# A new hand-written order for the start of a fused attention and squared-ReLU kernel, without its second set of zero matmuls

## The chip, the cores and the metric

The kernel runs on one core of one Trainium2 chip. The metric is device time in microseconds for one launch; the time before is the median of three runs. A profile is one further execution, with its own time.

The engines are named as the profile names them: PE (matmuls), ACT, DVE and POOL (elementwise work), SP (which here only issues DMAs). POOL also issues all loads that change fp32 to bf16 on the way.

## What is computed

```python
# attention: batch 4, 8 heads, sequence 768, head size 64; n_global 8, n_local 96
scores = (q @ k.T) / sqrt(64) + bias          # bias: minus slope times distance, per head
scores = where(first 8 keys, or 0 <= i - j < 96, scores, -1e9)
a = softmax(scores);  attn = a @ v
x = attn.transpose(0, 2, 1, 3).reshape(3072, 512)
# two-layer block
out = relu(x @ w_in) ** 2 @ w_out             # w_in 512 x 2048, w_out 2048 x 512
```

All inputs and the output are fp32 in DRAM; the matmuls run in bf16 and accumulate in fp32.

## The kernel before

**Tiles and stages.** The 3072 tokens are 24 tiles of 128, six to a batch element, and two tiles make a block (12 blocks). For each tile j the kernel transposes q and k (`tr.0.j`, `tr.1.j` on PE, then the copies `T.0.j`, `T.1.j` out of PSUM), computes the scores (`sc.j.0`) of its own keys and of the tile before, takes exp (`exp.j.odd.g` on ACT), multiplies with v (`pv.j.half`), normalizes (`norm`, DVE) and transposes x (`trx.j` on PE, copy `xT.j`). From tile 8 on the transposes are DMAs on SP's queue. For tiles 0 to 2 the bias is put into the scores by matmuls (`bias.j.0`); for later tiles the exps are multiplied with a table (`mul`, DVE). The eight global keys and rows of v are copied from tile to tile within a batch element (`gk.j`, `gv.j`).

**The two layers.** Blocks 0 and 1 do the first layer plainly (`s1.block.step`, then `relu` and `sq`). Blocks 2 to 11 do it with seven instead of eight products over sums of halves (`h.block.group.p1` to `p7`, with copies `u` on ACT and additions `c` on DVE). Blocks 1 to 11 do the second layer the same way (`s2.block.p1` to `p7`, with sums `sum`, weight sums `wsum`, `isum`, copies `part`, outputs `o`, stores `st`); block 0 does it plainly (`s2.0.step.half`).

**Who sets the order.** The program is recorded as a list of named operations, and the text ORDER (lines 57 to 161) gives the order in which they are issued, one word each. `name@V`, `@A`, `@P` chooses DVE, ACT or POOL; digits behind a colon are the PSUM banks (eight in all) that the operation opens. Each engine works through its own instructions in this order, and semaphores make it wait for data and for buffers. Operations on different engines overlap; a word's place counts only against words on the same engine. `ld.*` and `load.j` are loads on POOL's queue, `st.*` and `T.8` to `T.23` stand on SP's queue.

**The start.** q and k of tile 0 come as fp32 over SP (lines 313 to 324) and are transposed as fp32. Eight matmuls on zeros (lines 371 and 372, NWARM) run before anything has landed. A second set of eight (NKEEP, lines 529 to 533, the word `warm`) stands between tile 0's q and k transposes. POOL's first loads are piece 3 of w_in, k and q of tile 1, v of tile 0. q and k of tiles 1 to 5, all of v up to tile 5, w_in (ten transfers) and w_out (eight) are loaded once; `load.6` and later bring v, q and k of one tile each.

**The places that the change touches**, with the lines of the kernel before: `open_sc` and `emit_sc` (568, 590), which give the score matmuls their banks; the dependencies of `pv` (758 to 760); the ring of copies `u` (897, 973); and the last block's final product `p3`, which is cut into 192 and 64 columns, each with its own addition `o.11.p3` and store (1200, 1261, 1281).

```python
for i in range(NWARM):
    nc.tensor.matmul(out=banks[7], lhsT=zero[:, :P], rhs=zero, start=True, stop=True)
```

## Time and profile before

| | us |
|---|---|
| time, median of 3 runs | 199.85 |
| the three runs | 199.13, 199.85, 200.0 |
| the profiled execution's own time | 199.37 |
| its span, from its first to its last instruction | 197.6 |
| PE busy in the span | 191.9 |
| DVE busy | 173.2 |
| ACT busy | 163.0 |
| POOL busy | 80.4 |

The span is what the trace covers; 199.37 - 197.6 = 1.77 us of the execution's time lie around it. Times in the rows are microseconds from the span's start. A row of the timeline gives start, duration, engine, line, operation, output and inputs with their shape, the count of merged instructions, and in brackets the idle time before it with what ended that. A matmul's duration includes its passage through the array, so two matmuls in a row overlap: the distance between their starts is what one of them costs, not the duration. An engine that the row names as a releaser is the one that was last to arrive.

### The profile page before, as it was taken

The page shows a single profiled execution, that of the slowest core. Times are in us where ns is not written, and L with a number is a line of the kernel's source. Part 1 is how long each engine was busy: PE and PEld are TensorE (multiplying, and loading weights), DVE is VectorE, ACT ScalarE, POOL GpSimd, SP SyncE. Part 2 cuts the span into 40 slices and gives each one's busy share as a digit, 9 for nine tenths or more (in the row PEclk, how much of TensorE's full clock was granted, in tenths as well). Part 3 has the DMA queues.
Part 4 walks back from the last instruction along what each step waited for, and adds up shares of the span by engine and source line. Part 5 has one row for each costly group of instructions (what it writes and reads, how often), then busy time and mean ns, then how long its engine had stood idle before and what let it go on. Part 6 is the DMA issues. An engine that isn't in the chain of part 4 may idle for free.

```text
span 197.6 us, 6777 instructions
## 1 busy us (share of the span) xinstructions
PE 191.9 (97%) x2776; PEld 169.6 (86%) x2776; DVE 173.2 (88%) x423; ACT 163.0 (82%) x335; POOL 80.4 (41%) x101
## 2 busy tenths in 40 slices
...
GB/s 127 153 158 171 181 181 185 182 202 159 139 209 191 75 200 88 145 174 210 151 129 203 114 124 194 160 121 92 136 81 116 154 55 56 27 30 163 0 106 106
DMA packets 111857, 26.91 MB, mean 136 GB/s; under 512 B 103379, under 2 KB 109011, under 8 KB 111827
## 3 DMA queue, kind: packets, MB, share of 16 engines
...
q8 instruction: 21, 0.34, 0.6%
...
## 4 chain that ended last, share of the span: by engine, by line
PE 95%; DVE 2%; issue 1%; ACT 0%; DVEq 0%
PE bank L1212 35%; PE bank L950 32%; PE bank L1061 7%; PE bank L599 6%; PE bank L748 5%; PE bank L1339 4%; PE bank L372 2%; PE bank L506 2%; PE bank L532 1%; DVE qkT L433 1%; PE bank L816 1%; PE bank L579 0%; ACT qkT L429 0%; DVE o L1287 0%; DVE v L433 0%
## 5 line engine op out<-in xcount | busy, mean ns | idle before, releaser
L1015 ACT ACTIVATE hs<-hr 128x512 bf16<-128x512 f32 x72 | 44.8, 641 | 5.1 <-DVE hr L995 4.7
L665 ACT ACTIVATE esc<-bank 128x512 bf16<-128x512 f32 x78 | 42.9, 614 | 1.3 <-PE bank L599 1.0
L1212 PE MATMUL bank<-wsum,hsum 128*128 128x256 bf16 x264 | 36.2, 273 | 0.0
L1212 PEld LDWEIGHTS <-hsum 128*128 128x128 bf16 x360 | 32.1, 98 | 4.1 <-issue 0.5
L995 DVE CUSTOM_DVE_ANT_0 hr<-bank,early 128x512 f32<-128x512 f32 x45 | 30.4, 685 | 2.5 <-PE bank L950 1.5
L950 PEld LDWEIGHTS <-win 128*128 128x128 bf16 x480 | 29.7, 98 | 1.0
L950 PEld LDWEIGHTS <-qk_first 128*128 128x128 bf16 x480 | 29.7, 98 | 1.0
L429 ACT COPY early<-bank 128x512 f32<-128x512 f32 x42 | 24.5, 591 | 3.6 <-PE bank L950 3.3
L690 DVE TENSOR_TENSOR at<-esc,E 128x1024 bf16<-128x1024 bf16 x39 | 26.7, 696 | 0.1
L1212 PEld LDWEIGHTS <-hs 128*128 128x128 bf16 x264 | 24.0, 98 | 2.6
L310 POOL DMA_DIRECT2D qk<-in_q_dram x18 | 16.0, 890 | 21.9 <-DMA qkT<-qk 20.6
L1212 PE MATMUL bank<-wout,hs 128*128 128x256 bf16 x176 | 24.9, 273 | 0.0
L310 POOL DMA_DIRECT2D v<-in_v_dram x18 | 16.0, 888 | 18.3 <-DVE v L480 14.9
L950 PE MATMUL bank<-xT,win 128*128 128x128 bf16 x320 | 23.4, 219 | 0.0
L431 POOL COPY v<-v 8x520 bf16<-8x520 bf16 x8 | 5.7, 718 | 43.3 <-PE bank L748 43.3
L950 PE MATMUL bank<-xs,qk_first 128*128 128x128 bf16 x320 | 22.8, 219 | 0.0
L779 DVE TENSOR_TENSOR x<-bank,rs 128x256 bf16<-128x256 f32 x48 | 20.4, 425 | 1.7
L865 ACT ACTIVATE hr<-bank 128x512 f32<-128x512 f32 x33 | 19.4, 598 | 1.3 <-PE bank L950 0.4
L748 PE MATMUL bank<-v,at 128*128 128x65 bf16 x352 | 17.8, 193 | 0.0
L1287 DVE TENSOR_TENSOR o<-bank,part 128x256 f32<-128x256 f32 (+2 forms) x34 | 13.8, 410 | 3.3 <-PE bank L1212 3.2
L429 ACT COPY part<-bank 128x256 f32<-128x256 f32 x29 | 10.9, 375 | 7.1 <-PE bank L1212 6.9
L310 POOL DMA_DIRECT2D qk<-in_k_dram x18 | 16.1, 897 | 0.9 <-DMA win<-in_moe_w_in_dram 0.5
...
## 6 DMA issues: line engine op xcount, KB each, us to landing
out_dram<-o SPq DMA_DIRECT2D x22, 256.0 KB, 2.5
v<-in_v_dram POOLq DMA_DIRECT2D x24, 128.0 KB, 5.6
qk<-in_q_dram POOLq DMA_DIRECT2D x18, 128.0 KB, 5.0
qk<-in_k_dram POOLq DMA_DIRECT2D x18, 128.0 KB, 5.8
wout<-in_moe_w_out_dram POOLq DMA_DIRECT2D x8, 256.0 KB, 8.5
win<-in_moe_w_in_dram POOLq DMA_DIRECT2D x6, 256.0 KB, 6.9
qk_first<-in_k_dram POOLq DMA_DIRECT2D x5, 128.0 KB, 5.6
qk_first<-in_q_dram POOLq DMA_DIRECT2D x5, 128.0 KB, 5.7
```

The source lines that it names most:

```text
L310: nc.gpsimd.dma_start(out=dst, in_=src)
L429: nc.scalar.copy(dst, src)
L665: nc.scalar.activation(out=tiles[tag, j, g][:, odd], in_=tiles.pop(("sc", j, odd, g)).rearrange("p a c -> p (a c)"), func=Act.Exp, scale=s ...
L690: nc.vector.tensor_mul(at, tiles.pop(("esc", j, g)), bias)
L748: nc.tensor.matmul(out=po[:, hi, :], lhsT=tiles["at", j, g][:, odd, at * P : (at + 1) * P], rhs=v_sb[kj][:, h, :], start=(i == 0), stop=(i ...
L779: nc.vector.tensor_tensor(out=x[:, 4 * hf : 4 * hf + 4, :], in0=po[:, :, :D], in1=rs.to_broadcast([P, 4, D]), op=Alu.mult,)
L865: nc.scalar.activation(dst, src, Act.Relu)
L950: nc.tensor.matmul(out=tiles["h", blk, g, bank][:, n], lhsT=left_[:, s, k], rhs=right_[:, k], start=opens and n == 0 and k == 0, stop=k == ...
L995: nc.vector._custom_dve(TENSOR_ADD_SAT, out=hr, in0=src, in1=tiles.pop(("u", blk, g, i)), s0=float("inf"), s1=0.0,)
L1015: nc.scalar.activation(hs, hr, Act.Square)
L1061: nc.tensor.matmul(out=hT[:, c, cols], lhsT=w_in_sb[s][:, kt, c * P : (c + 1) * P], rhs=tiles["xT", blk][:, kt, cols], start=(kt == 0), st ...
L1212: nc.tensor.matmul(out=tiles["acc", blk, bank][:, cols], lhsT=left_[:, s], rhs=right_[:, cols], start=first and s == 0, stop=s == NSTEP - ...
```

## The change

The second set of zero matmuls goes. In ORDER, all words up to tile 7's transposes stand in a new order: POOL's loads begin with q and k of tile 1 and follow the tiles, with w_in and w_out behind; the bias matmuls, transposes, scores, exps and first-layer products of blocks 0 and 1 are interleaved anew, and some copies, ReLUs and squares change between ACT, DVE and POOL (the copies `gv.2` to `gv.4` leave POOL). Behind that the order of the engines' work stays nearly as it was, with other bank numbers and with loads and stores grouped at fewer places.

In the code: the score matmuls can open several banks from an offset; a copy `u` takes a buffer from a list of free ones and gives it back; `pv` of tile j also waits for the load of v of tile j-1; and in the last block both additions of `p3` wait until both cuts of the product are done (`done[-1]`), so that the matmuls of the second cut stand before the first addition. Lines of the changed kernel lie about seven lower than before.

```diff
--- before
+++ after
@@ -55,109 +55,109 @@
 ORDER = """
-tr.0.0:0 warm:7 tr.1.0:1 T.1.0@V bias.0.0:23 T.0.0@A sc.0.0 ld.win.3.0 exp.0.0.0 ld.k.1 tr.1.1:4 bias.1.0:5670 T.1.1@V ld.q.1
-tr.0.1:1 ld.v.0 exp.0.1.0 T.0.1@V sc.1.0 exp.1.0.1 pv.0.0:2 ld.q.2 tr.0.2:3 norm.0.0 ld.k.2 T.0.2@V ld.k.3 exp.1.1.1
-pv.0.1:4 tr.1.2:1 bias.2.0:7203 ld.v.1 norm.0.1 exp.1.1.0 ld.q.3 tr.1.3:6 gk.1@A T.1.2@A sc.2.0 exp.1.0.0 T.1.3@V
-ld.k.4 pv.1.0:4 ld.v.2 gk.2@V exp.2.1.0 exp.2.1.1 norm.1.0 trx.0:1 xT.0@A ones.6 pv.1.1:5 tr.0.3:6 T.0.3@V exp.2.0.0
-tr.1.4:2 ld.win.6.0 sc.3.0:4361 ld.q.4 norm.1.1 ld.v.3 trx.1:7 gv.1@V exp.2.0.1 exp.3.0.0 pv.2.0:5 exp.3.1.0 exp.3.0.1
-T.1.4@V xT.1@V pv.2.1:0 ld.k.5 ld.win.2.0 exp.3.1.1 gk.3@A ld.win.2.1 norm.2.0 s1.0.3:2 mul.3.0 s1.0.6:4 ld.win.4.0
-tr.0.4:7 ld.q.5 ld.v.4 norm.2.1 mul.3.1 relu.0.6@A s1.0.3#2 gv.2@P pv.3.0:3 norm.3.0 trx.2:5 T.0.4@A pv.3.1:6
-ld.win.1.0 norm.3.1 ld.win.0.1 xT.2@A sc.4.0:1047 exp.4.1.1 exp.4.1.0 tr.1.5:3 T.1.5@A s1.0.2:5 trx.3:6 xT.3@V
-ld.win.0.0 ld.win.5.0 s1.0.2#2 s1.0.2#3 s1.0.2#4 relu.0.3@V exp.4.0.1 ld.v.5 gv.3@P exp.4.0.0 gk.4@V sq.0.6@V
-relu.0.2@A s1.1.3:7 ld.win.7.0 relu.1.3@A load.6 s1.1.6:0 mul.4.1 tr.0.5:6 mul.4.0 sq.0.3@V s1.1.2:3 T.0.5@A ld.wout.3
-pv.4.0:2 ld.wout.1 sq.0.2@V sc.5.0:4157 ld.wout.0 s1.0.4:6 relu.1.2@A exp.5.1.1 s1.0.1:3 sq.1.3@A exp.5.0.0 relu.0.4@V
-s1.1.4:7 ld.wout.2 norm.4.0 pv.4.1:4 gv.4@P norm.4.1 sq.0.4@A load.7 exp.5.1.0 sq.1.2@A relu.1.4@A s1.0.0:6 gate.9
-ld.wout.4 mul.5.0 s1.0.0#2 sq.1.4@A s1.0.0#3 s1.1.5:2 trx.4:1 exp.5.0.1 relu.1.6@V s1.1.1:4 ld.wout.5 s1.0.1#2
-relu.1.1@A E0.1 mul.5.1 relu.1.5@A pv.5.0:7 s1.1.7:0 s1.1.0:5 sq.1.1@V norm.5.0 ld.wout.6 E0.0 sq.1.5@V tr.1.6:4
-sq.1.6@A pv.5.1:2 relu.1.7@A tr.0.6:7 s1.0.0#4 norm.5.1 xT.4@A sq.1.7@A h.2.0.p2:0 ld.wout.7 T.1.6@V h.2.1.p2:1
-trx.5:2 xT.5@V relu.1.0@A sq.1.0@A gate.14 h.2.0.p1:5 xs.2.0 s1.0.5:4 sum.1.2 s1.0.7:2 relu.0.1@A xs.2.1 gate.10
-sum.1.0 sum.1.1 relu.0.0@A T.0.6@A sc.6.0:36 wsum.0.0 sum.1.3 sq.0.0@A sq.0.1@A s2.0.0.0:7 relu.0.7@A s2.0.1.0 load.9
...
+ld.q.1 ld.k.1 ld.k.2 ld.q.2 ld.v.0 ld.q.3 ld.k.3 ld.v.1 ld.k.4 ld.v.2 ld.q.4 ld.v.3 ld.win.3.0 ld.win.6.0 ld.win.2.0
+ld.win.2.1 ld.k.5 ld.q.5 ld.v.4 ld.win.0.0 ld.win.0.1 tr.0.0:0 T.0.0@V ones.6 load.6 ld.v.5 ld.win.4.0 ld.win.1.0
+ld.win.7.0 ld.win.5.0 ld.wout.3 ld.wout.0 ld.wout.1 ld.wout.2 load.7 ld.wout.4 ld.wout.5 ld.wout.6 ld.wout.7 tr.1.0:1
+T.1.0@A bias.0.0:23 tr.0.1:4 T.0.1@V sc.0.0 exp.0.0.0 exp.0.1.0 tr.1.1:5 T.1.1@V bias.1.0:6701 tr.1.2:4 T.1.2@A sc.1.0
+gk.1@V exp.1.0.0 exp.1.1.0 exp.1.1.1 tr.0.2:2 T.0.2@V bias.2.0:5346 pv.0.0:2 pv.0.1:7 sc.2.0 exp.1.0.1 norm.0.0
+exp.2.1.1 norm.0.1 tr.0.3:1 exp.2.1.0 tr.1.3:0 trx.0:2 T.1.3@V exp.2.0.1 pv.1.0:7 pv.1.1:6 gate.9 exp.2.0.0 gk.2@V
+xT.0@V tr.1.4:3 T.0.3@V T.1.4@A norm.1.0 gv.1@V sc.3.0:0241 exp.3.1.0 pv.2.0:5 norm.1.1 norm.2.0 pv.2.1:7 tr.0.4:3
+gk.3@A exp.3.0.1 norm.2.1 exp.3.0.0 trx.1:6 trx.2:2 T.0.4@V sc.4.0:5470 exp.3.1.1 mul.3.0 gv.2@A pv.3.0:3 xT.1@A
+gk.4@A mul.3.1 norm.3.0 pv.3.1:1 s1.0.3:6 s1.0.3#2 exp.4.0.0 norm.3.1 exp.4.1.1 xT.2@A exp.4.0.1 trx.3:5 xT.3@A
+gate.11 relu.0.3@V s1.0.6:3 exp.4.1.0 mul.4.0 s1.0.2:0 s1.1.3:1 gv.3@A s1.0.2#2 sq.0.3@V tr.1.5:2 s1.0.2#3 relu.0.6@V
+s1.0.2#4 tr.0.5:7 relu.0.2@V s1.1.6:6 pv.4.0:5 T.1.5@V T.0.5@A sq.0.6@A sc.5.0:4307 mul.4.1 relu.1.3@A pv.4.1:2
+norm.4.0 exp.5.1.0 s1.0.0:1 s1.0.0#2 exp.5.0.1 exp.5.1.1 exp.5.0.0 sq.1.3@V sq.0.2@V s1.0.0#3 s1.0.0#4 s1.1.0:5
+relu.1.0@A sq.1.0@A s1.1.2:3 norm.4.1 tr.0.6:0 relu.1.2@A relu.1.6@A tr.1.6:7 load.9 load.8 T.8 trx.4:4 gv.4@V T.0.6@A
+mul.5.0 pv.5.0:2 mul.5.1 pv.5.1:5 xT.4@V T.1.6@V gate.13 sc.6.0:34 E0.1 norm.5.0 gate.15 sq.1.6@V norm.5.1 relu.0.0@V
+sq.0.0@A s1.0.4:6 s1.0.1:7 s1.0.1#2 s1.1.1:0 sq.1.2@A exp.6.0.0 relu.0.1@A sq.0.1@A s1.1.7:2 h.2.1.p1:5 relu.0.4@A
+relu.1.7@A exp.6.1.0 E0.0 trx.5:1 relu.1.1@V sq.1.1@A s1.1.5:3 sq.1.7@V s1.0.7:7 xT.5@V mul.6.0 relu.0.7@A relu.1.5@V
+sq.1.5@A h.2.1.p2:6 gate.14 wsum.0.0 wsum.1.0 h.2.0.p1:0 gate.10 wsum.2.0 s2.0.0.1:2 s2.0.1.1 xs.2.0 sq.0.4@A s1.1.4:4
+s2.0.0.0:1 s2.0.2.1 s2.0.1.0 xs.2.1 s1.0.5:7 relu.1.4@A sq.1.4@A sum.1.0 tr.1.7:3 gate.12 tr.0.7:4 load.10 isum.0.0
+s2.0.2.0 isum.1.0 isum.0.1 relu.0.5@A s2.0.3.1 isum.1.1 u.2.1.1@A c.2.1.c11 pv.6.0:7 T.1.7@A s2.0.3.0 s2.0.4.0
+u.2.0.1@A norm.6.0 isum.3.0 xs.2.2 sq.0.7@A sum.1.1 h.2.0.p6 sum.1.2 sq.0.5@A h.2.0.p2:3 c.2.0.c11 isum.3.1 h.2.1.p6
+s2.0.5.0 u.2.0.2@A s2.0.4.1 s2.0.5.1 u.2.1.2@A h.2.0.p7 u.2.0.3@A s2.0.6.0 T.0.7@A s2.0.6.1 s2.0.7.1 o.0.1@A st.0.1
+T.9 load.12 T.10 load.11 sc.7.0:6743 exp.7.0.0 wsum.0.1 s2.0.7.0 wsum.2.1 s2.1.p2.0:2 s2.1.p2.1 s2.1.p1.0:6 exp.7.1.0
...
-part.11.p6@A s2.11.p2.0:6 st.10.1 s2.11.p2.1 sum.11.2#2 o.11.p2 s2.11.p7.0 s2.11.p7.1 part.11.p7@A sum.11.3 s2.11.p5.0
-s2.11.p5.1 o.11.p5 st.11.1 st.11.0 sum.11.3#2 s2.11.p4.0 s2.11.p4.1 o.11.p4@A st.11.1#2 s2.11.p3.0 s2.11.p3.1
-s2.11.p3.0#2 o.11.p3 s2.11.p3.1#2 st.11.0#2 o.11.p3#2 st.11.0#3
+sum.11.2 s2.11.p6.1 part.11.p6@A s2.11.p2.0:6 s2.11.p2.1 sum.11.2#2 o.11.p2 s2.11.p7.0 s2.11.p7.1 part.11.p7@A
+sum.11.3 s2.11.p5.0 s2.11.p5.1 o.11.p5 st.11.1 st.11.0 sum.11.3#2 s2.11.p4.0 s2.11.p4.1 o.11.p4@A st.11.1#2 s2.11.p3.0
+s2.11.p3.1 s2.11.p3.0#2 s2.11.p3.1#2 o.11.p3 st.11.0#2 o.11.p3#2 st.11.0#3
@@ -276,7 +276,6 @@
     NSUM = 2
     NAT, NESC = 4, 2
     NWARM = 8
-    NKEEP = 8
     NLATE, NO = 2, 3
     CUT = 3 * d_model // 4
     TWO = (0, 2)
@@ -526,12 +525,6 @@
             first_reads.append(tr)
             if not fp:
                 qk_users[slot(j)].append(tr)
-        if j == 0:
-            def emit_warm(e):
-                for _ in range(NKEEP):
-                    nc.tensor.matmul(out=psum(), lhsT=zero[:, :P], rhs=zero, start=True, stop=True)
-
-            plan.op(("warm",), {"PE": 0.216 * NKEEP}, emit_warm, key=base)
         if j >= JQK:
             def emit_dT(e, j=j, T_=T_):
                 nc.sync.dma_start_transpose(
@@ -565,8 +558,8 @@
             ]
             return [(*x, odd) for x in every if x[0] in gs for odd in range(2)]
 
-        def open_sc(gs, j=j):
-            for n, (g, odd) in enumerate((g, odd) for g in gs for odd in range(2)):
+        def open_sc(gs, at=0, j=j):
+            for n, (g, odd) in enumerate(((g, odd) for g in gs for odd in range(2)), at):
                 tiles["sc", j, odd, g] = psum(n).rearrange("p (a c) -> p a c", a=4)
 
         def emit_bias(e, gs, j=j, first=first, todo=todo, open_sc=open_sc):
@@ -587,13 +580,14 @@
                 )
                 opened.add((odd, g))
 
-        def emit_sc(e, gs, j=j, todo=todo, open_sc=open_sc):
+        def emit_sc(e, gs, at=0, j=j, todo=todo, open_sc=open_sc):
             if isinstance(gs, list):
                 for f, gs in gs:
-                    f(e, gs)
+                    f(e, gs, at)
+                    at += 2 * len(gs)
                 return
             if j >= NBIAS:
-                open_sc(gs)
+                open_sc(gs, at)
             for g, pair, at, kt, odd in todo(gs):
                 half = slice(odd * D, (odd + 1) * D)
                 nc.tensor.matmul(
@@ -757,7 +751,7 @@
             g = 0 if first else hf
             deps = [*mul[g], land["v", j]]
             if not first:
-                deps.append(glob.get(("v", j - 1)))
+                deps += [glob.get(("v", j - 1)), land["v", j - 1]]
             p_ = plan.op(
                 ("pv", j, hf), {"PE": 0.13 if first else 0.25}, emit_pv, deps=deps,
                 key=base + 2 + 2 * hf,
@@ -895,7 +889,7 @@
                 )
 
     u_ring = [early[:, i] for i in range(3)] + [const([P, 4 * P], FP32, f"u_{i}") for i in range(3, NU)]
-    u_next = [0]
+    u_free = list(u_ring)
 
     def first_seven(blk):
         husers = hs_users[blk] = []
@@ -971,8 +965,7 @@
                 cu = []
 
                 def emit_u(e):
-                    u = u_ring[u_next[0] % NU]
-                    u_next[0] += 1
+                    u = u_free.pop(0)
                     any_copy(e, u, tiles["h", blk, g, bank].rearrange("p a c -> p (a c)"))
                     tiles["u", blk, g, i] = u
 
@@ -992,9 +985,9 @@
                     hr = work.tile([P, 2, 2 * P], FP32, name="hr", tag="hr", bufs=NHR).rearrange("p a c -> p (a c)")
                     src = tiles["h", blk, g, bank].rearrange("p a c -> p (a c)")
                     if i:
-                        nc.vector._custom_dve(
-                            TENSOR_ADD_SAT, out=hr, in0=src, in1=tiles.pop(("u", blk, g, i)), s0=float("inf"), s1=0.0,
-                        )
+                        u = tiles.pop(("u", blk, g, i))
+                        nc.vector._custom_dve(TENSOR_ADD_SAT, out=hr, in0=src, in1=u, s0=float("inf"), s1=0.0)
+                        u_free.append(u)
                     else:
                         any_relu(e, hr, src)
                     tiles["hr", blk, g, name] = hr
@@ -1258,7 +1251,7 @@
                 copied[name] = (o, cu)
             else:
                 sub, n, other = {"p2": (0, 0, "p1"), "p5": (1, 1, "p7"), "p4": (1, 0, None), "p3": (0, 1, "p6")}[name]
-                for o, cols in zip(done, cuts):
+                for o, cols in zip([done[-1]] * len(cuts), cuts):
                     later.append((blk, name, bank, sub, n, cols, other, o, key, copied, users, prev, ousers, stores))
                 if name == "p5":
                     continue
```

172 lines of the change are left out of this document (84 added, 88 removed).

## The prediction

> **What bounds the kernel now.** First the page's busy line and its chain, then the windows, then the chain in order of time for the spacing of matmuls.
>
> ```profile
> span 197.6 us, 6777 instructions
> PE 191.9 (97%) x2776; PEld 169.6 (86%) x2776; DVE 173.2 (88%) x423; ACT 163.0 (82%) x335; POOL 80.4 (41%) x101
> ...
> PE 95%; DVE 2%; issue 1%; ACT 0%; DVEq 0%
> ```
> ```profile
> 10.00:15.00 5.00, 4.33 (x73) 3.55 (x70) 2.73 (x8) 3.54 (x9) 5.00 (x8) 1.00 2.33 160
> 15.00:20.00 5.00, 4.66 (x94) 4.26 (x91) 4.56 (x19) 4.88 (x11) 5.00 (x8) 1.00 2.06 171
> 20.00:25.00 5.00, 5.00 (x87) 4.52 (x84) 4.25 (x12) 4.60 (x10) 5.00 (x8) 1.00 1.84 180
> 25.00:30.00 5.00, 5.00 (x80) 4.56 (x78) 3.33 (x9) 4.35 (x9) 3.89 (x6) 1.00 1.81 180
> 30.00:60.00 30.00, 30.00 (x372) 24.22 (x371) 29.18 (x69) 26.11 (x53) 17.61 (x22) 1.00 1.68 179
> 21.00:193.90 172.90, 172.90 (x2547) 156.09 (x2544) 159.59 (x369) 148.77 (x304) 60.23 (x73) 1.00 1.20 134
> ```
> ```profile
> 44.43 1.30 PE bank L1339 x6
> ...
> 93.10 3.13 PE bank L950 x56
> ...
> 161.76 2.18 PE bank L1212 x20
> ```
> The window columns are busy time of PE, PEld, DVE, ACT, POOL. From 21.0 to 193.9 us PE has no gap, and its matmuls follow each other at 0.056 us for 128 columns, 0.109 for 256 and 0.217 for 512, so those 172.9 us are work, not disguised waiting. What can be saved lies before 21 us and behind 193.9. How PE starts:
>
> ```profile
> 1.19 3.60 PE L372 MATMUL bank<-early 128*128 128x512 bf16 x8 [1.19 <-DVE early L361]
> ...
> 4.58 1.06 PE L506 MATMUL bank<-ident,plain 128*128 128x128 f32 x4
> ...
> 5.43 2.62 PE L532 MATMUL bank<-early 128*128 128x512 bf16 x8
> ...
> 6.71 0.15 PEld L532 LDWEIGHTS <-early 128*128 128x128 bf16 x1 [0.28 <-issue]
> 7.03 0.53 PEld L532 LDWEIGHTS <-early 128*128 128x128 bf16 x3 [0.16 <-issue]
> ...
> 7.89 0.60 PE L506 MATMUL bank<-ident,plain 128*128 128x128 f32 x4
> ...
> 9.28 0.40 PE L599 MATMUL bank<-qkT 64*128 64x128 bf16 x8 [0.34 <-DVE qkT L433]
> ...
> 11.62 0.23 PE L599 MATMUL bank<-qkT 64*128 64x128 bf16 x2 [0.52 <-DVE qkT L433]
> ...
> 16.65 0.23 PE L599 MATMUL bank<-qkT 64*128 64x128 bf16 x2 [0.29 <-DVE qkT L433]
> ...
> 21.04 0.23 PE L599 MATMUL bank<-qkT 64*128 64x128 bf16 x2
> ```
> The eight matmuls of L372 stand 0.43 us apart ((4.58-1.19)/8), twice the later 0.217; weight loads of L532 are still far apart at 6.71 and stand close from 7.03 on. So PE runs at half speed until about 6.9 us, after 5.7 us without a gap. The page's clock row shows none of this; the spacing does. The rows of L599 are the scores of tiles 0, 1, 3 and 4 (9.28, 11.62, 16.65, 21.04).
>
> From the end of the k transposes (8.3) to 21.0 the order holds 10.5 us of PE work, counted from its matmuls by the spacings above (with 0.55 to 0.67 for a score block and 0.24 for a probabilities-times-v block of eight), in 12.7 us: 2.2 us are waits. After those transposes PE thus has 10.5 + 172.9 = 183.4 us of work.
>
> **The zero matmuls.** They take PE from 5.43 to 7.89, 2.46 us. But the transposes behind them need tile 0's k:
>
> ```profile
> plain<-in_q_dram SPq DMA_DIRECT2D x1, 256.0 KB, 3.1
> plain<-in_k_dram SPq DMA_DIRECT2D x1, 256.0 KB, 6.0
> win<-in_moe_w_in_dram POOLq DMA_DIRECT2D x1, 256.0 KB, 5.7
> ...
> 1.25 0.56 SPq L319 DMA_DIRECT2D plain<-in_k_dram  x1
> 1.34 0.89 POOL L307 DMA_DIRECT2D win<-in_moe_w_in_dram  x1 [0.17 <-issue]
> 2.22 0.90 POOL L307 DMA_DIRECT2D qk_first<-in_k_dram  x1
> 3.10 0.90 POOL L307 DMA_DIRECT2D qk_first<-in_q_dram  x1
> ```
> k landed at 1.25 + 6.0 = 7.25, beside the first piece of w_in at 1.34 + 5.7 = 7.04; if that stays, removing the matmuls gains 0.64 us. q, issued 0.6 us ahead of POOL's first transfer, took 3.1, so k can be no earlier than about 4.4. In the changed kernel the first POOL transfer is a q tile, half as large. I take 6.4 (estimate, nearer to the late end, because the sharing stays), so transposes from 6.4 to 7.1, the first of them still at half speed, against 8.3: 1.2 us earlier. A gap-free PE would then end its work at 7.1 + 183.4 = 190.5 instead of 193.9. That is the most the change could give, 3.4 us; the rest is what takes it back.
>
> **The clock.** With the zeros gone PE idles from 5.43 to about 6.4. I take it that speed still doubles near 6.9, since PE has worked 4.2 us before the gap. The other bound: the 5.7 us of gapless work start again at 6.4, half speed until 12.1. That is a rival below.
> The Trainium skill, "TensorE: Matmul & The Clock Gate", section "Part 1: The HAM clock gate", says the clock is released after one busy window of about 3.4 us, in windows that run free of the kernel's start, so that the place of the change varies from run to run. The trace agrees as far as it goes: 5.7 us lies between one window and two. By that page the gap of 1 us can spoil a window in some runs, and then the rival's price is due.
>
> **The loads.** POOL issues them in order, and they land evenly:
>
> ```profile
> qk_first<-in_k_dram POOLq DMA_DIRECT2D x5, 128.0 KB, 5.6
> ...
> qk<-in_k_dram POOLq DMA_DIRECT2D x2, 128.0 KB, 7.5
> ...
> 33.42 0.88 POOL L310 DMA_DIRECT2D qk<-in_k_dram  x1
> ...
> 36.33 0.70 POOL L307 DMA_DIRECT2D wout<-in_moe_w_out_dram  x1 [0.56 <-DMA wout<-in_moe_w_out_dram]
> 37.61 0.71 POOL L307 DMA_DIRECT2D wout<-in_moe_w_out_dram  x1 [0.58 <-DMA wout<-in_moe_w_out_dram]
> ```
> A q, k or v tile costs the queue 0.87 us (issues 0.87 apart at a steady 5.6 to land), a 256 KB weight piece 1.28 (two issues, each released by a landing), half a piece about 0.7. Tile 7's k came at 33.42 + 7.5 = 40.9. The new order starts with a 0.87 transfer in place of a 1.28 one: first landing 6.4 to 6.7 (7.04 less 0.4, and some sharing). Behind it and up to tile 7's k stand 21 tiles, 10 pieces and 4 halves: 18.3 + 12.8 + 2.8 = 33.9, so 40.3. Ahead of the transposes of that k the new order has 30.6 us of work after tile 0's transposes, so 183.4 - 30.6 = 152.8 remain: no end before 40.3 + 152.8 = 193.1. The same sum gives 192.6 for w_in piece 5 (32.6 + 160.0) and 191.4 for piece 6. Loads alone hold back 2.6 of the 3.4 us.
>
> **The order of work up to tile 7.** What must keep up is ACT and DVE:
>
> ```profile
> 17.31 2.12 ACT L665 ACTIVATE esc<-bank 128x512 bf16<-128x512 f32 x4
> ...
> 18.33 0.62 POOL L431 COPY v<-v 8x520 bf16<-8x520 bf16 x1
> ...
> 20.14 0.58 ACT L429 COPY qkT<-bank 128x512 bf16<-128x512 bf16 x1
> ```
> Four exps take 2.12, so one costs ACT 0.5. Between tile 1's first exp and the copy of tile 6's transposed q the new order gives ACT 36 instructions, about 17 us at such paces, while PE has 19.4 us of work from tile 0's transposes to tile 6's scores (before, 28.0 with about 23 on ACT). Walking the queues from 6.4: scores of tile 1 at 9.6 (11.62), of tile 3 at 14.0 (16.65, held by the DVE copy of tile 3's q), of tile 4 at 16.9 (21.04, though with less work ahead), of tile 6 at 28.8, because ACT does relu and square of block 1 before that copy. At tile 6's scores 19.4 us of counted work lie behind 7.1, so 2.3 us of waits have come up: end at 190.5 + 2.3 = 192.8. Loads give 193.1; the later decides. 193.9 - 193.1 = 0.8 us gained, 1.1 if the loads are 0.3 sooner; I take 1.0.
> The three copies of the global v rows that POOL gave up before tile 5 (0.62 each) go to ACT twice and DVE once, and are in that walk; POOL's loads are free of them. In all 16 instructions come to DVE and 12 leave it, about 2.3 us; DVE's idle time from 10 to 30 us (2.27 + 0.44 + 0.75 + 1.67 = 5.1) covers them. If that cover is gone they cost up to 2.3.
>
> **The last bank.**
> ```profile
> 194.16 0.36 DVE L1287 TENSOR_TENSOR o<-bank,part 128x192 f32<-128x192 f32 x1 [0.84 <-PE bank L1212]
> 194.57 0.28 PE L1212 MATMUL bank<-wout,hsum 128*128 128x64 bf16 x4 [0.45 <-DVE o L1287]
> 194.88 0.22 DVE L1287 TENSOR_TENSOR o<-bank,part 128x64 f32<-128x64 f32 x1 [0.37 <-PE bank L1212]
> ```
> PE waits 0.45 for DVE and DVE then 0.37 for PE. With all matmuls first, the 192-column add starts some 0.1 later and the 64-column one follows at once, 194.7 instead of 194.88; but the two stores issue one after the other. Between -0.1 and +0.3, I take 0.1 gained. The list of free u buffers, the added wait for tile j-1's v (landed long before) and the loads and stores that stand elsewhere in POOL's and SP's queues after 45 us I cost at nothing: PE's gap-free stretch covers them; without that cover a transfer that comes late would cost its lateness in full.
>
> **Sum.** 1.0 + 0.1 = 1.1 off a span of 197.6: 196.5. The profiled execution took 199.37, 1.77 around its span; so 198.3 by it. The median shown is 199.85, 0.48 above that execution; I give the result half of that: 198.5.
>
> **Rivals.**
> 1. *The clock stays low* until 9 to 12 us (0.27). For it: PE needed 5.7 gapless us. Against: 4.2 us come before the gap. Tile 1's biases and scores then run at half speed and its scores begin at about 11.0, not 9.6, with the exps and all behind them 1.4 later, over the loads' bound: end 194.3, 0.4 later than now and 0.1 back at the tail: 199.7 by the profiled run; with 12.1 another 1.0, 200.7.
> 2. *Nothing comes through* (0.13): k of tile 0 still lands at 7.25 and every load half a microsecond later than I reckon, or the exps' chain costs 1 more. For it: the new order meets its loads with 0.1 to 0.6 us to spare, where the old one had 0.7 and more. 199.2 to 199.9.
> 3. *DVE becomes the bound* (0.15), the one that makes it slower. Between 30 and 60 us it is busy for 29.18 of 30 now. If the 2.3 us are not worked off before 30, only 0.8 of idle time is left to take them, and PE, whose banks DVE frees, falls 1.5 behind: 200.9. It decides as soon as DVE shows 30.0 of 30 and PE rows are released by DVE there.
>
> **Chances.** The forecast (0.45) has its own range of 197.7 to 199.0, from the 3.4 us that are not to be had in full and the bounds of k's landing. The measurement tells apart about 0.5%, 1.0 us: faster means below 198.85. From the forecast 0.38 lies there, with 0.02 from rival 2: 0.40. Slower than 200.85: most of rival 3 (0.13) and the late part of rival 1 (0.06), 0.19. The rest, 0.41, is no change. Range 197.7 to 200.7.
>
> **What would show it.** Right: PE's first fp32 k transposes near 6.4; weight loads 0.06 apart by 8 us; scores of tiles 1, 3, 4 and 6 at 9.6, 14.0, 16.9 and 28.8; PE without idle time after 29; tile 7's k transposes near 40.3; no PE wait on DVE at the end. Wrong: bias matmuls of 256 columns 0.21 apart after 9 us (rival 1), PE idle on loads or on ACT between 17 and 45 (rival 2), PE released by DVE between 30 and 60 (rival 3). A landing of tile 0's k before 6 or a first POOL landing before 6 would make it faster than I say.

## The result, and the profile after

| | before | after |
|---|---|---|
| median, us | 199.41 (199.13 to 200.0, 6 runs) | 201.67 (200.69 to 203.18, 6 runs) |
| profiled execution, us | 199.37, span 197.6 | 202.56, span 200.8 |

The ratio of the times is 1.0113, 95% interval 1.0065 to 1.016: the changed kernel is about 2.3 us slower. 198.5 was forecast, with 200.7 as the upper end. The profiled execution stands 0.9 above the median, so it shows somewhat more loss than a usual run.

First the page of the changed kernel: span, busy time of the engines, and the shares of its chain.

```profile
span 200.8 us, 6760 instructions
...
PE 190.5 (95%) x2768; PEld 168.0 (84%) x2768; DVE 176.5 (88%) x427; ACT 163.2 (81%) x335; POOL 78.0 (39%) x97
...
PE 58%; DMA 15%; POOL 12%; DVE 10%; issue 2%; ACT 1%; DVEq 0%; POOLq 0%
```
Before, PE was 95% of that chain and no transfer stood in it. Now transfers are 15% and POOL, which issues them, is 12%. The start of PE, in order of time:

```profile
4.31 0.60 PE L505 MATMUL bank<-ident,plain 128*128 128x128 f32 x4
5.11 0.66 PE L505 MATMUL bank<-ident,plain 128*128 128x128 f32 x4 [0.20 <-DMA plain<-in_k_dram]
5.60 0.61 PE L572 MATMUL bank<-pb,early 128*128 128x128 bf16 x8
...
8.20 0.23 PE L593 MATMUL bank<-qkT 64*128 64x128 bf16 x2
```
Tile 0's k is transposed at 5.11, where 7.89 was the old time and 6.4 the forecast, and the scores of tile 1 begin at 8.20 instead of 11.62. The start is better than predicted by more than a microsecond. The same engine's waits, the largest first (us in total, times, longest), and the windows (busy time of PE, PEld, DVE, ACT, POOL, then clock, DMA share and GB/s):

```profile
PE bank L944 <- DVE xs L916: 2.0, 2, 1.8
PE bank L371 <- DVE early L360: 1.2, 1, 1.2
PE bank L742 <- DMA v<-in_v_dram: 0.9, 2, 0.5
PE bank L593 <- ACT qkT L428: 0.8, 2, 0.6
PE bank L1054 <- DMA win<-in_moe_w_in_dram: 0.5, 1, 0.5
PE bank L1332 <- DMA wout<-in_moe_w_out_dram: 0.5, 1, 0.5
PE bank L810 <- DVE x L773: 0.3, 1, 0.3
PE bank L505 <- DMA plain<-in_k_dram: 0.2, 1, 0.2
PE bank L505 <- ACT at L659: 0.2, 1, 0.2
PE bank L742 <- DVE at L684: 0.2, 1, 0.2
```
```profile
5.00:45.00 40.00, 36.59 (x519) 30.15 (x520) 31.95 (x86) 31.86 (x64) 33.44 (x42) 1.00 1.86 176
...
45.00:60.00 15.00, 15.00 (x197) 12.15 (x195) 14.60 (x31) 12.32 (x26) 5.09 (x7) 1.00 1.77 175
60.00:90.00 30.00, 28.06 (x441) 25.40 (x439) 26.47 (x65) 25.70 (x55) 12.24 (x14) 1.00 1.39 136
90.00:130.00 40.00, 39.77 (x639) 36.60 (x637) 38.16 (x92) 36.29 (x76) 15.36 (x18) 1.00 1.42 150
```
The kernel before, in the same window from 5 to 45 us, and the one line of its waits that falls into it:

```profile
5.00:45.00 40.00, 38.65 (x526) 31.43 (x525) 30.09 (x79) 32.16 (x66) 35.78 (x45) 1.00 1.88 177
```
```profile
PE bank L599 <- DVE qkT L433: 1.1, 3, 0.5
```
Two places lose time. Between 5 and 45 us PE is idle for 3.4 us (40.00 - 36.59) where it was idle for 1.35, and the transfers run at 176 GB/s against 177: the DMA engines moved nearly the same bytes in the same time, in another order. Of the waits listed up to 45 us, 2.1 us are for transfers (L742, L1054, L1332 and the k of L505) and 1.3 for ACT and DVE; before, none was for a transfer and 1.1 were for DVE. What is new is the waiting for transfers. Between 60 and 90 us PE has a gap of 1.9 us where the kernel before had none.

To see where the lead goes, add to the start of a step the PE work that stands from it to the end, counted from the order by the spacings of the prediction. While PE does not wait, this sum stays the same; each wait raises it.

| step | before: start, sum | after: start, sum |
|---|---|---|
| scores of tile 1 | 11.62, 193.5 | 8.20, 189.9 |
| scores of tile 3 | 16.65, 194.3 | 13.26, 190.9 |
| scores of tile 4 | 21.04, 194.6 | 16.47, 192.3 |
| scores of tile 6 | 38.59, 194.7 | 29.16, 193.9 |
| transposes of tile 7's k | 42.61, 194.6 | 40.92, 194.5 |
| first product with w_out piece 4 | 43.28, 194.6 | 43.45, 195.1 |
| scores of tile 8 | 59.03, 194.8 | 58.64, 195.2 |
| last bank's products | 193.18, 194.9 | 196.31, 198.1 |

The lead of 3.6 us at tile 1's scores is 0.1 at tile 7's k and turned into a loss of 0.5 by 44 us; another 2.7 follow behind 60 us, 1.8 of them at one place. This is one execution: e1, e2, e3, e5 and e6 below begin with the same order of work, and in theirs the first product with w_out piece 4 starts anywhere from 42.57 to 43.43, so the 0.5 at 44 us is uncertain by almost a microsecond. The first part is told by the landings (issue plus time to landing of each transfer) against the first use on PE:

| load | before: landed, used | after: landed, used |
|---|---|---|
| v of tile 2 | 15.59, 17.44 | 14.34, 14.38 |
| w_in piece 1 | 26.02, 27.59 | 30.99, 31.03 |
| k of tile 7 | 41.16, 42.61 | 40.87, 40.92 |
| w_out piece 4 | 42.51, 43.28 | 43.41, 43.45 |

Of the loads that PE uses before 45 us, the old order leaves each one 0.75 us or more; in the new order eleven are used within 0.05 us of their landing. The chain of waits of the changed kernel names the last of them, and the gap behind 60 us:

```profile
33.48 9.93 DMA wout<-in_moe_w_out_dram
...
73.48 7.09 DMA xT<-x
```
The w_out piece issued at 33.48 lands at 43.41, and PE's row for L1332 waits for it. The DMA transpose of x of tile 9 takes 7.09 us; DVE's xs waits for it, then PE (L944, 1.8 us, at 81.7). For the transposes of x in SP's queue between 60 and 110 us the view of the tile xT gives the time from issue to landing, first before, then after:

```profile
DMA to landing us min/median/max: 2.5/4.6/5.1
```
```profile
DMA to landing us min/median/max: 2.4/2.5/7.1
```
Tile 9's was the fast one before (2.5) and is the slow one now. POOL's and SP's issues around it, first after:

```profile
70.57 0.88 POOL L309 DMA_DIRECT2D qk<-in_q_dram  x1 [6.22 <-DMA qkT<-qk]
71.43 0.88 POOL L309 DMA_DIRECT2D qk<-in_k_dram  x1
72.30 0.91 POOL L309 DMA_DIRECT2D v<-in_v_dram  x1
73.18 0.90 POOL L309 DMA_DIRECT2D qk<-in_q_dram  x1
```
```profile
71.52 1.39 SPq L530 DMA_TRANSPOSE qkT<-qk  x1
73.48 1.55 SPq L834 DMA_TRANSPOSE xT<-x  x1
```
and POOL's first one before:

```profile
74.29 0.87 POOL L310 DMA_DIRECT2D qk<-in_q_dram  x1 [6.73 <-DMA qkT<-qk]
```
In the changed order tile 12's transposes stand ahead of tile 8's transpose of x; they land 3.4 us sooner (70.01 against 73.44) and release tile 15's loads at 70.57, so that tile 9's transpose, at 73.48, comes behind four loads. Before, it was issued at 72.53, ahead of the first at 74.29.

### The profile page after: what moved, and what is told of

Same layout as the page of the kernel before. It is cut to its first block, busy times and chain, and to the rows that moved or that the text cites. A ratio compares the mean times of both kernels' runs of the same rounds, so it can differ in the third digit from the quotient of the medians.

```text
span 200.8 us, 6760 instructions
## 1 busy us (share of the span) xinstructions
PE 190.5 (95%) x2768; PEld 168.0 (84%) x2768; DVE 176.5 (88%) x427; ACT 163.2 (81%) x335; POOL 78.0 (39%) x97
## 3 DMA queue, kind: packets, MB, share of 16 engines
HBM read 27.26 MB, written 6.29 MB: 167 GB/s over the span
## 4 chain that ended last, share of the span: by engine, by line
PE 58%; DMA 15%; POOL 12%; DVE 10%; issue 2%; ACT 1%; DVEq 0%; POOLq 0%
PE bank L1205 26%; PE bank L944 24%; DMA xT<-x 6%; DMA wout<-in_moe_w_out_dram 5%; POOL qk_first L306 4%; DMA win<-in_moe_w_in_dram 4%; POOL win L306 3%; PE bank L593 3%; PE bank L742 3%; POOL v L306 3%; DVE hr L989 2%; PE bank L1332 2%; DVE xs L916 2%; DVE hsum L1160 2%; DVE at L684 2%
## 5 line engine op out<-in xcount | busy, mean ns | idle before, releaser
L1008 ACT ACTIVATE hs<-hr 128x512 bf16<-128x512 f32 x71 | 44.1, 643 | 4.8 <-DVE hr L989 4.4
L944 PEld LDWEIGHTS <-qk_first 128*128 128x128 bf16 x480 | 29.5, 98 | 3.4 <-issue 1.9
L944 PEld LDWEIGHTS <-win 128*128 128x128 bf16 x480 | 29.9, 98 | 1.1
L428 ACT COPY early<-bank 128x512 f32<-128x512 f32 x44 | 26.0, 596 | 4.4 <-PE bank L944 4.2
L309 POOL DMA_DIRECT2D qk<-in_q_dram x18 | 15.9, 885 | 28.8 <-DMA qkT<-qk 26.5
L944 PE MATMUL bank<-xs,qk_first 128*128 128x128 bf16 x320 | 22.6, 219 | 2.0 <-DVE xs L916 2.0
L944 PE MATMUL bank<-xT,win 128*128 128x128 bf16 x320 | 23.6, 219 | 0.0
L859 ACT ACTIVATE hr<-bank 128x512 f32<-128x512 f32 x30 | 17.6, 594 | 2.2 <-PE bank L1054 0.8
L430 POOL COPY v<-v 8x520 bf16<-8x520 bf16 x4 | 3.0, 748 | 41.8 <-PE bank L742 41.8
L742 PE MATMUL bank<-v,at 128*128 128x65 bf16 x352 | 17.0, 193 | 1.1 <-DMA v<-in_v_dram 0.9
L742 PEld LDWEIGHTS <-at 128*128 128x128 bf16 x352 | 14.9, 98 | 2.4 <-issue 1.1
L1054 PE MATMUL bank<-xT,win 128*128 128x256 bf16 (+1 forms) x160 | 15.7, 251 | 0.5 <-DMA win<-in_moe_w_in_dram 0.5
```

The source lines that it names most:

```text
L309: nc.gpsimd.dma_start(out=dst, in_=src)
L428: nc.scalar.copy(dst, src)
L742: nc.tensor.matmul(out=po[:, hi, :], lhsT=tiles["at", j, g][:, odd, at * P : (at + 1) * P], rhs=v_sb[kj][:, h, :], start=(i == 0), stop=(i ...
L859: nc.scalar.activation(dst, src, Act.Relu)
L944: nc.tensor.matmul(out=tiles["h", blk, g, bank][:, n], lhsT=left_[:, s, k], rhs=right_[:, k], start=opens and n == 0 and k == 0, stop=k == ...
L1008: nc.scalar.activation(hs, hr, Act.Square)
```

## The experiments

After the two traces two causes stood to be tested: the loads up to 45 us set PE's pace in the new order (L below), and a DMA transpose is late among loads (first A, then C). Their rivals: the loss moves to any other transfer (B), ACT and DVE set the pace (D). Each run gives the ratio to the kernel before, timed beside it on one chip. In the diffs a line of words is a piece of ORDER.

### Where the transfers behind tile 7 stand

**e1, e2, e3** put transfers of the changed kernel back behind the compute words of the kernel before: all (e1), SP's alone (e2), POOL's alone (e3). The core of e1:

```diff
-o.0.1@A st.0.1 T.9 load.12 T.10 load.11
...
+norm.6.1 c.2.0.c21@A load.12 wsum.3.0
...
+o.1.p2 h.2.1.p4 T.9 c.2.1.c22
...
-o.1.p3 st.1.0 T.12 load.15 load.13 gk.8@A
...
+s2.2.p7.0 c.3.1.c22 T.12 s2.2.p2.1
...
+h.3.1.p3 c.3.1.c12 load.15 h.3.0.p4
```
A load that is recorded ahead of the transposes of the tile whose buffer it fills replaces that tile's data. In e1 tile 9's transposes take tile 12's q and k; in e2 those of tiles 9, 11, 12, 13 and 17 take the tile loaded next into their buffer; in e3 those of tiles 21 and 22 take what was there before.

> The changed kernel with one part undone: behind tile 7's transposes the loads from tile 11 on, the stores and the DMA transposes from tile 9 on stand again behind the same compute steps as in the kernel before; the front, the missing zero matmuls and the tail stay as changed. Theory A (the regrouped transfers make the DMA transpose for tile 9 late, 7.1 us instead of 2.5, and PE loses 2.6 us between 60 and 110 us): tile 9's transpose takes under 4 us, PE has no gap at 81 us, and the time falls to 0.995 to 1.003 of the kernel before (198.5 to 200 us). Theory B (the changed kernel has no slack left at any transfer, so the loss comes up somewhere else): the time stays at 1.008 of the kernel before or more.

> As the run with all transfers put back, but only the stores and DMA transposes of SP's queue; POOL's loads stay at their changed places. Theory A1 (what delays the transpose is what stands ahead of it in SP's own queue): the whole gain of the run with all transfers back, 0.995 to 1.003. Theory A2 (it is the loads of tiles 12 to 15 that POOL now issues at 63 to 78 us, in the same stretch): no gain, 1.008 or more, and tile 9's transpose still takes over 5 us.

> As the run with all transfers put back, but only POOL's loads; SP's stores and DMA transposes stay at their changed places. Theory A1 (SP's queue): no gain, 1.008 or more. Theory A2 (POOL's loads in the same stretch): 0.995 to 1.003 and tile 9's transpose under 4 us.

**e4** is the reverse in the kernel before. Tile 10's loads came to stand between the two transposes of tile 7, whose k is replaced, and one column of tile 12's v is zeroed behind its load.

```diff
-s2.0.3.1 tr.0.7:3 tr.1.7:6 gate.15
+s2.0.3.1 tr.0.7:3 load.10 tr.1.7:6 gate.15
...
+o.1.p3 st.1.0 T.12 load.15 load.13
```

> The kernel before with that one part of the change: the loads from tile 10 on, the stores and the DMA transposes from tile 9 on stand behind the compute steps of the changed kernel; front, zero matmuls and tail are those of before. Theory A: slower by 1.5 to 2.6 us, 1.008 to 1.013, with a PE gap near tile 9's MoE step. Theory B: the old front leaves slack, so 0.998 to 1.004.

| run | ratio | interval | transpose of tile 9's x, us |
|---|---|---|---|
| e1 | 1.0111 | 1.0042 to 1.018 | 3.6 |
| e2 | 1.0699 | 1.0638 to 1.076 | 2.5 |
| e3 | 1.0133 | 1.0098 to 1.0168 | 6.9 |
| e4 | 1.0876 | 1.0829 to 1.0922 | |

e1 took the late transpose away, as theory A said, and won nothing: tile 12's loads were issued ahead of tile 9's transposes, which then waited for them, and tile 8's transposes among them took 8.0 us (4.4 after, 3.7 before). A as a whole falls by its own number, but the run is no clean test. e3 stands: with POOL's words alone back, tile 9's transpose still takes 6.9, because POOL's loads wait for tile 12's transposes, whose place SP's order sets. e2 and e4 do not tell the theories apart: in e2 PE waited three times for 2 to 4 us for DMA transposes that its order brings late, in e4 once for 12 us for tile 10's k, which stands ahead of tile 7's second transpose.

**e5** is e1 with `T.9 load.12` in this order. **e6** moves three words only:

```diff
-o.1.p3 st.1.0 T.12 load.15 load.13 gk.8@A
+o.1.p3 st.1.0 gk.8@A
...
-gv.8@A mul.9.0 xT.8 st.1.1 T.11
+gv.8@A mul.9.0 xT.8 T.12 load.15 load.13 st.1.1 T.11
```

> The first run once more with one word set right: there tile 12's loads stood ahead of tile 9's DMA transposes, so that these read tile 12's q and k and waited for them; here they stand behind. The loads from tile 11 on, the stores and the DMA transposes from tile 9 on stand where the kernel before has them; front and tail are those of the change. Theory C (a DMA transpose that is issued among POOL's loads lands behind them; the changed places bring that about at tile 9): tile 9's transpose takes under 4 us, what is left of the loss is the front's 0.5 us, and the ratio is 1.000 to 1.005. Theory B (no slack anywhere, the loss moves to another transfer): 1.008 or more.

> The changed kernel with three words moved: tile 12's DMA transposes and the loads of tiles 15 and 13 that wait for them stand behind tile 8's transpose of x, as in the kernel before, not ahead of it. Theory C: tile 12's transposes land 3 us later, so those loads are issued from about 74 us instead of 70.6, tile 9's transpose at 73.5 meets an emptier queue and takes 2.5 to 4 us instead of 7.1; PE's gap of 1.8 us at 81 us is gone: ratio 1.001 to 1.005. Theory B: another transfer is late instead, 1.008 or more.

e5 gave 1.0085 (1.005 to 1.0121), e6 1.0089 (1.006 to 1.0118). Tile 9's transpose took 3.6 and 3.5 us and PE's gap at 81 us was gone in both, so the mechanism is as theory C has it; but the time fell by only 0.25%, and the intervals overlap that of the changed kernel. Both theories missed in size, and how much of the 1.8 us comes through to the end is not settled: e3's profiled execution, which stands at its median, has the gap too (1.6 us at 81.5), while in e5 half of it came back as a wait of 0.9 us for tile 13's x at 107 us, of which more below.

### The loads up to 45 us

**e7** moves two loads that have time to spare:

```diff
             def emit_load(e, j=j):
-                load_v(j)
+                if j == 9:
+                    load_v(7)
+                if j not in (6, 7):
+                    load_v(j)
                 load_part(0, j)
                 load_part(1, j)
+                if j == 7:
+                    load_v(6)
```

> The changed kernel with two loads moved in POOL's queue: tile 6's v, which has 16.9 us to spare, goes behind tile 7's k, and tile 7's v, which has 14.4, ahead of tile 9's loads. Theory L (in the changed kernel the loads set PE's pace up to 45 us): the weight piece for s1.0.1 lands 0.9 us earlier, tile 7's k 1.7 and the fifth piece of w_out 0.9 earlier, and PE comes to 45 us 0.5 to 0.9 us earlier; the time falls by as much, ratio 1.005 to 1.008. Rival D (ACT and DVE set the pace there): PE's place at 45 us changes by less than 0.2 us, 1.010 to 1.014.

1.0052 (1.003 to 1.0074). The w_in piece landed 1.05 us earlier, tile 7's k 1.4, the w_out piece 1.9; the sum of the table above at tile 8's scores is 194.35 instead of 195.2. PE's waits in this kernel:

```profile
PE bank L598 <- ACT qkT L428: 1.0, 2, 0.8
PE bank L949 <- DVE xs L921: 0.5, 1, 0.5
PE bank L815 <- DVE x L778: 0.3, 1, 0.3
PE bank L747 <- DVE at L689: 0.2, 1, 0.2
```
No load stands among them any more. Theory L holds, and rival D falls as the main account, though a wait of 0.8 us for ACT's copy at tile 6 stays: with 0.87 to 1.75 us less ahead of the late loads more than half of the loss is gone. It is the largest effect of one edit, but the intervals of e6 and e7 overlap, and two things qualify it. The gain is not that of the front alone: only one load was issued ahead of tile 9's transpose here, it took 4.5 us instead of 7.1, and the gap at 81 us is gone as in e6. And the sums compare one execution with one: e5 and e6, whose loads up to 45 us stand as in the changed kernel, have about 195.0 and 194.6 at tile 8's scores.

**e17** gives PE more to do ahead of the loads: the eight zero matmuls put back into the changed kernel.

```diff
-ld.wout.5 ld.wout.6 ld.wout.7 tr.1.0:1
+ld.wout.5 ld.wout.6 ld.wout.7 warm:7 tr.1.0:1
```

> The changed kernel with the eight zero matmuls of the kernel before put back between tile 0's q and k transposes; nothing else differs. They delay PE's first bias matmuls by 1.7 us at full speed to 2.9 at half. Theory L (the loads set the pace up to 45 us): PE then waits less for the loads, is at the same place by 25 us, and the time stays within 0.2 % of the changed kernel, 1.009 to 1.014. Rival (what PE does first sets the end): 1 to 2 us slower, 1.016 to 1.025.

1.0126 (1.0075 to 1.0177), against 1.0113 without them. The scores of tile 1 begin at 9.71, 1.5 us later than at 8.20. At tile 6's scores 0.7 us of that is left (29.89 against 29.16), at w_out piece 4 0.3 (43.71 against 43.45), and the end hardly moves; of PE's waits for loads 0.2 us are left:

```profile
PE bank L599 <- ACT qkT L428: 0.8, 2, 0.7
PE bank L950 <- DVE xs L922: 0.7, 1, 0.7
PE bank L599 <- DVE qkT L432: 0.3, 1, 0.3
PE bank L816 <- DVE x L779: 0.3, 1, 0.3
PE bank L505 <- DMA qk<-in_k_dram: 0.2, 1, 0.2
```
PE was not back at the same place by 25 us, as expected, but by 44 us most of the 1.5 us had taken the place of waits for loads. The zero matmuls gain or cost nothing in this order that an interval of 0.5% to either side can show.

**e8** leaves them out of the kernel before (`NKEEP = 8` becomes 0).

> The kernel before with the eight zero matmuls left out and nothing else changed. Theory L: tile 0's k still lands at 7.2 us beside the first piece of w_in, PE starts its transposes 0.6 us earlier, and as the loads have 0.75 us or more to spare most of it comes through: 0.997 to 0.999. Rival K (the clock): with PE idle from 5.4 to 7.2 us the clock doubles later, and it is 1.000 to 1.005.

0.9998 (0.9972 to 1.0024): neither. PE starts its k transposes 1.0 us sooner, at 6.89, but behind an idle 1.25 us, and what follows runs at half speed:

```profile
6.89 1.11 PE L506 MATMUL bank<-ident,plain 128*128 128x128 f32 x4 [1.25 <-DMA plain<-in_k_dram]
7.80 1.06 PE L579 MATMUL bank<-pb,early 128*128 128x128 bf16 x8
8.79 0.61 PE L599 MATMUL bank<-qkT 64*128 64x128 bf16 x8
```
The eight 128-column matmuls of L579 take 1.06, where the changed kernel has 0.61. By tile 1's scores (11.70, before 11.62) the gain is gone: rival K's mechanism, with no loss left over.

### Mends put together, and what caps them

**e9** joins e6 and e7 and moves tile 18's loads to their old place; **e12** adds one more word.

```diff
-h.5.1.p3 gv.13@P load.17 load.18 q.5.1.c22@V
+h.5.1.p3 gv.13@P load.17 q.5.1.c22@V
...
-exp.15.0.1 sum.5.1 h.6.0.p5:0
+exp.15.0.1 sum.5.1 load.18 h.6.0.p5:0
```
```diff
-norm.4.1 tr.0.6:0 relu.1.2@A relu.1.6@A
+norm.4.1 tr.0.6:0 T.0.6@A relu.1.2@A relu.1.6@A
...
-trx.4:4 gv.4@V T.0.6@A mul.5.0
+trx.4:4 gv.4@V mul.5.0
```

> The changed kernel with three mends together: tile 12's transposes and the loads of tiles 15 and 13 behind tile 8's transpose of x; the v tiles 6 and 7 later in POOL's queue; and tile 18's loads where the kernel before has them. If the two losses are separate (loads up to 45 us, transposes among loads behind it), the gains seen alone, 0.24 and 0.61 %, add up: 1.000 to 1.004. If both mends only took away the same wait, or if what is left is ACT's and DVE's, it stays at 1.005 to 1.009.

> The kernel with the three mends, and ACT's copy of tile 6's transposed q moved ahead of its relus of block 1's steps 2 and 6, behind the transposes that it copies. If ACT's order holds tile 6's scores (PE loses 0.8 to 1.0 us there at 29 us), the scores start 0.5 us or more sooner and the time falls by 0.2 to 0.4 % against the three mends alone. If the loads hold PE right behind it anyway, it stays within 0.1 % of them.

e9: 1.0040 (1.0012 to 1.0068). The gains seen alone, 0.24 and 0.61% off 1.0113, would give 1.0028; but e9 lies inside e7's interval, and e7 takes the late transpose away too, so that the two losses are separate is not shown. e12: 1.0054 (1.0027 to 1.0081): moving the copy made tile 6's scores 0.3 us earlier (29.08) and the time no better; ACT's order there is not what decides.

**e11** takes the kernel before, without zero matmuls, and mends its load order (with the edit of e7):

```diff
-sc.0.0 ld.win.3.0 exp.0.0.0 ld.k.1
+sc.0.0 exp.0.0.0 ld.k.1
...
-tr.1.4:2 ld.win.6.0 sc.3.0:4361
+tr.1.4:2 ld.win.3.0 ld.win.6.0 sc.3.0:4361
```

> The kernel before, its order of work kept, with the zero matmuls left out, the first piece of w_in (11 us to spare) moved back to just ahead of the second, and the v tiles 6 and 7 later as in the changed kernel's mend. Theory L: tile 0's k lands at about 5.1 us, every load up to 16 us comes 1.3 us sooner, and those from tile 6's k to the w_out pieces 0.9 sooner; PE gains 0.5 to 1.0 us: 0.995 to 0.998. Rival D (ACT and DVE set the pace of the old front): 0.999 to 1.002.

0.9999 (0.997 to 1.0028), though PE was ahead: tile 3's scores at 14.57 instead of 16.65, tile 4's at 20.20 instead of 21.04. PE lost 0.4 us of that at 90.1, in a wait for ACT, and the chain of waits shows another place:

```profile
99.54 5.57 DMA xT<-x
```
That is tile 13's x, issued behind two of these loads:

```profile
98.36 0.87 POOL L310 DMA_DIRECT2D v<-in_v_dram  x1
99.22 0.88 POOL L310 DMA_DIRECT2D qk<-in_q_dram  x1
100.09 0.89 POOL L310 DMA_DIRECT2D qk<-in_k_dram  x1
```
PE waits for its product at 105.9, and so it does at 106 to 108 us in e5 to e9 and e12 and in the changed kernel (108.9), by 0.2 to 1.4 us. In the kernel before the same transpose takes 4.9 us and lands 0.1 us before its use: a limit right behind the one in front.

**e13, e14, e15** hold POOL back before those loads, in e9, e11 and the kernel before. The copy waits for tile 13's x.

```diff
     touch = const([1, 16], FP32, "touch")
+    pgate = const([1, 8, 16], BF16, "pgate")
...
             def emit_load(e, j=j):
+                if j == 17:
+                    nc.gpsimd.tensor_copy(out=pgate, in_=tiles["x", 13][:1, :, :16])
```

> The changed kernel with the three mends, and POOL made to wait for tile 13's x (a copy of 128 values of it into a spare row) before it issues the loads of tiles 17 and 18, so that tile 13's DMA transpose of x is issued beside the first of them and not among five. Theory F (that transpose is the next limit): it takes 3 to 4.5 us instead of 6, PE's step of 0.7 us at 106 us goes, and the ratio falls from 1.004 to 1.000 to 1.002. Rival (what is left is ACT's and DVE's in the front, or the held loads are late themselves): 1.003 or more.

> The kernel before without zero matmuls and with its front loads mended, and with POOL held in the same way before the loads of tiles 17 and 18. Theory F: the 0.8 us that it is ahead at 20 us come through to the end, 0.994 to 0.997 of the kernel before. Rival: another stage caps them, 0.998 to 1.002.

> The kernel before with nothing but the hold before the loads of tiles 17 and 18. Theory F: it has only 0.3 us to gain there, 0.997 to 1.000. Rival: the held loads make a later transfer late, 1.003 or more.

| run | ratio | interval | transpose of tile 13's x, us |
|---|---|---|---|
| e9 | 1.0040 | 1.0012 to 1.0068 | 6.0 |
| e13 = e9 and hold | 1.0023 | 0.9995 to 1.0052 | 4.2 |
| e11 | 0.9999 | 0.997 to 1.0028 | 5.6 |
| e14 = e11 and hold | 0.9983 | 0.9961 to 1.0004 | 4.2 |
| e15 = before and hold | 1.002 | 0.9992 to 1.0047 | 5.3 |

In e13 and e14 PE no longer waits at 106 us, and both come 0.16 to 0.17% lower, less than F expected and less than the intervals tell apart; for e15 nothing is gained, and its profiled transpose was no faster. Against the changed kernel itself the mends together are clear: e13 leaves the new order of PE's, ACT's and DVE's work as it is and differs in when transfers are issued, and 1.0113 (1.0065 to 1.016) became 1.0023 (0.9995 to 1.0052), two intervals that do not overlap. e14, PE's waits of over 0.2 us:

```profile
PE bank L373 <- DVE early L362: 1.2, 1, 1.2
PE bank L1069 <- DMA win<-in_moe_w_in_dram: 0.8, 1, 0.8
PE bank L607 <- DVE qkT L434: 0.8, 2, 0.5
PE bank L1220 <- DVE o L1295: 0.4, 1, 0.4
```
Its one large wait is again for a load. It is the fastest kernel tried, 199.04 us against 199.47, but its interval still holds 1.

**e18** keeps the zero matmuls in e14 (`NKEEP = 8`).

> The kernel before with its front loads mended and the hold (the best so far, 0.998), with its zero matmuls kept. If the zero matmuls cost nothing while the loads hold PE, 0.997 to 0.9995; if their time reaches the end, 1.000 to 1.004.

1.0016 (0.9986 to 1.0046), 0.3% above e14, in the range that was expected if their time reaches the end: here they seem to cost something, though the intervals overlap.

**e10, e16** bring the order of e6's three words, reversed, into the kernel before; e16 also gives one copy to ACT, as the change does.

```diff
-gate.12 c.2.0.c21@A load.12 pv.7.0:2
+gate.12 c.2.0.c21@A load.12 load.11 pv.7.0:2
...
+xT.7@V o.1.p3 T.12 load.15 load.13
...
+q.3.1.c11@A norm.8.1 xT.8 T.11 load.14
```
```diff
-s2.2.p2.0:1 sum.2.2 gv.8@P q.3.1.c11@A
+s2.2.p2.0:1 sum.2.2 gv.8@A q.3.1.c11@A
```

> The kernel before with that order of transfers alone: tile 11's loads behind tile 12's, tile 12's DMA transposes and the loads of tiles 15 and 13 ahead of tile 8's transpose of x, tile 11's transposes and tile 14's loads right behind it; every load still stands behind the step that frees its buffer. Theory C: tile 9's transpose of x takes 5 to 7 us instead of 2.5, PE shows a gap of 1 us or more before 82 us, ratio 1.004 to 1.010. Rival (the old front leaves enough to spare for a late transpose): 0.998 to 1.002.

> The kernel before with tile 12's transposes and tile 15's and 13's loads ahead of tile 8's transpose, once more, and the copy of tile 8's global v rows on ACT and not on POOL, where it stood behind loads that wait. Theory C: PE's wait of 7.6 us for that copy is gone, tile 9's transpose takes 5 to 7 us, 1.003 to 1.010. Rival (the old front leaves enough to spare): 0.998 to 1.002.

e10: 1.0472 (1.0435 to 1.0508), for a reason that neither theory names:

```profile
76.64 0.55 PE L748 MATMUL bank<-v,at 128*128 128x65 bf16 x7 [7.57 <-POOL v L431]
```
POOL's copy of tile 8's global v rows stands behind loads that wait for tile 12's transposes. With it on ACT (e16) that gap is gone and the ratio is 1.0035 (1.0007 to 1.0063). Tile 9's transpose took 4.2 us there, with one load issued ahead of it, and PE did not wait for it in the profiled execution: the order costs a little in the old kernel, but the transpose did not take the 5 to 7 us expected.

## Why the prediction was wrong

- **k of tile 0 at 6.4, zero matmuls gone.** Better than said: k landed at 5.06, beside POOL's smaller first transfer, which landed at 5.80. The prediction held that a landing of either before 6 would make the kernel faster than forecast. It did not: a lead of PE at the start is mostly taken back in waits for loads by 44 us (e17).
- **The clock** (rival 1). Not seen in the changed kernel: PE's gap before its k is 0.20 us, and it runs at full speed from the first transposes. In part that is luck of the execution: its matmuls come twice as close from about 4 us on, those of e6 and e7, which start alike, from 6.7 and 6.9, and there the scores of tile 1 begin at 9.00 and 9.07, not 8.20. By tile 6's scores that no longer shows (28.89 and 29.30). e8 shows that the mechanism is real where the gap is 1.25 us: half speed until 10.1.
- **Scores of tiles 1, 3, 4, 6 at 9.6, 14.0, 16.9, 28.8.** 8.20, 13.26, 16.47, 29.16. At tile 6 the ACT copy holds PE as the walk of the queues said, but that the time there comes so close is luck: from tile 0's k to those scores the walk has 22.4 us and the trace 24.05; PE began 1.3 us sooner and waited 1.7 longer.
- **Loads: "no end before 193.1".** The mechanism was right, the term mis-sized, and this is the first step that failed. On the table's scale, where the kernel before stands at 194.6, tile 7's k at 40.3 gives 193.85 and its real landing of 40.87 gives 194.4; w_out piece 4, which I did not price, gives 195.1. It landed 2.5 us behind that k where pieces are 1.28 apart (e1: 1.28). So 0.8 of gain became 0.5 of loss. Pricing the piece would not have helped: 1.28 behind 40.3 gives it 193.2. What failed is the sum of even spacings. From the first landing to tile 7's k it has 33.9 us, and the trace has 35.07 (5.80 to 40.87); had I tried it on the kernel before, 22 tiles, 9 pieces and 4 halves, 33.5, stand against 34.12 there. (The 40.9 read for that k before is the median of two tiles; its own landing is 41.16.) I treated the bound as one transfer at its expected time, although the new order meets eleven loads with nothing to spare, and each that comes late adds its lateness.
- **"PE without idle time after 29".** Wrong: waits at 29.2 for the ACT copy that the walk has at 28.8, and beyond it at 31.0 for w_in piece 1, 43.4, 81.7 and 108.9.
- **"The loads and stores that stand elsewhere ... I cost at nothing: PE's gap-free stretch covers them".** The second step that failed. I read the stretch from 21 us as cover; it only meant that the old order was never late. Tile 9's transpose of x went from 2.5 to 7.1 us and cost PE 1.8 us in the profiled execution; e6, without it, came 0.25% lower in the median, with overlapping intervals. The sentence behind it, that without the cover lateness is paid in full, is what happened.
- **The last bank**, 0.1 gained: from the start of its last group of products to the span's end 4.42 us before (193.18 to 197.6) and 4.49 after (196.31 to 200.8). Nothing. The additions do end sooner, 1.58 us after that start instead of 1.93, but the last store is issued at 1.91 instead of 1.95, because it stands behind the other one, as the prediction feared.
- **Rivals.** Rival 1's end of 194.3 is 0.1 more than its own terms give (192.8 and 1.4). Rival 2 was nearest: it named the spare of 0.1 to 0.6 us, and priced it at half a microsecond. Rival 3 named the wrong engine: PE waits on DVE at L944, but DVE waits there for the transpose, and from 30 to 60 us DVE is less busy than before (26.68 us against 29.18).

What stays open: e13 is at 1.0023 with an interval that holds 1, so whether the new order of work itself costs a last 0.2% is not settled; nor is how the loss divides between the loads up to 45 us and the late transposes, nor why single transfers land up to 1.3 us off their spacing.
